# Top-k attention and a leaky-ReLU MLP in one kernel: the softmax chain one step shorter, the grouped PE work in the middle of a step, and eight small token chunks in place of two

## The chip, the cores and the metric

The kernel runs on one core of one Trainium2 chip. The metric is the device time of one execution in microseconds. The engines are named as in the profile: PE (TensorE, matrix products; PEld are its weight loads), DVE (VectorE), ACT (ScalarE), POOL (GpSimd) and SP (SyncE, which issues the DMAs). Each engine works off its own queue in order.

## The reference

For each of 8 batches and 8 heads, with 576 tokens and a head size of 64, every query row keeps its 32 largest scores, the rest are masked, and a softmax weighs the values. The result, as 4608 tokens of 512 numbers, goes through a two-layer MLP with a leaky ReLU.

```python
scores = scale * np.matmul(q, k.transpose(0, 1, 3, 2))          # 8 x 8 x 576 x 576
kth = np.partition(scores, -top_k, axis=-1)[..., -top_k:-top_k + 1]   # top_k = 32
mask = scores >= kth
scores = np.where(mask, scores, -1000000000.0)
scores = scores - np.max(scores, axis=-1, keepdims=True)
attn = np.exp(scores)
attn = attn / (np.sum(attn, axis=-1, keepdims=True) + 1e-09)
attn_out = np.matmul(attn, v)
...
h = x @ w_in                       # x: 4608 x 512, w_in: 512 x 2048
g = np.maximum(0.01 * h, h)
out = g @ w_out                    # w_out: 2048 x 512
```

Attention inputs are float32. The two weight matrices arrive as float64 words, and the kernel turns them into float32 itself.

## The kernel before

**Units and steps.** The attention is cut into 144 units. A unit is 128 query rows of a pair of heads (two row sets of 128 x 576 scores); per batch there are 16 such units and 2 that combine the 64 left-over rows of two pairs. The outer loop (L404) runs over steps. Step s works on unit(s) on DVE and on earlier units on the other engines. The list `steps` holds the first 4 units, then 6 empty steps (the gap, steps 4 to 9), then the remaining 140 units; so unit u from 4 on is worked on at step u + 6, and the last at step 149.

**What happens to a unit.** `scores` (PE L177, 4 matrix products into PSUM tiles psc, copied to s_sb by ACT L186). `top_k` on DVE: four rounds of MAX8 (L195) and three of MATCH_REPLACE8 (L198), two row sets each, cut into four slots, `slot(0)` to `slot(3)`. `mask` on POOL (L207 to L211), one step later. `exponents` and `sums` on ACT (L214, L219), two steps later. `reciprocals` on DVE (L223) and `normalize` on ACT (L226), late in that same step. `transpose_main` and `transpose_tail` on PE (L234, L240) with ACT copies to wT (L235, L241), three steps later (LAG = 3). `weigh_values` on PE (L262, tile po) with ACT copies to the token tiles x (L272), for two units at the end of every even step, between the `scores` of two coming units. s_sb has 6 buffers, psc one of each of its two, the transposes and po share two PSUM buffers.

**The MLP.** Tokens are taken in chunks, two of 128 and then 17 of 256. A chunk is ready when the values of all its units are weighed (`values_at`, `attended`). `mlp` is a generator: for each of 16 blocks of hidden features it multiplies a 128 x 128 block of w_in (stationary) with the x of the chunk (moving, 128 or 256 columns; tile ph, L282), applies the leaky ReLU on ACT into gT (L288), and then multiplies gT (stationary) with w_out (moving, 512 columns; tile pz, L294) per 128 tokens, copies (L301) and stores (L302). Every product in float32 shows as two MATMUL instructions in the profile. All MLP tiles share two PSUM buffers (`ps_ml`).

**The planner.** Everything is emitted in a fixed order (`manual_schedule`). At seven places in a step `mlp_steps(budget)` lets the generator emit pieces of the MLP until their cost, counted in matmul columns, has used up the budget. `slot_budget` sets the budget so that the backlog ends in the step in which the next chunk becomes ready: the MLP of a chunk is spread evenly over the steps until the next one is there.

**The weights.** In the gap DVE converts the sixteen 1 MB pieces of weights with help from ACT (`convert_weights`, L110 to L126); three slots of each gap step start one conversion and finish an older one.

The order of the calls in one step of the kernel before, which the change rearranges, is in the loop at the end of what follows.

Of the kernel before, what the change touches and what calls it, by code (L numbers as in the profile page):

```python
# [8 lines left out]
F32 = mybir.dt.float32  # L9
U32 = mybir.dt.uint32  # L10
AF = mybir.ActivationFunctionType
# [6 lines left out]
def kernel(  # L18
# [27 lines left out]
    WCH = 1024  # L46
    LEFT = S % P
    assert D == 64 and S == 576 and HP == 4 and B % 2 == 0 and LEFT == 64
    CHUNKS = [128] * 2 + [256] * 17
    assert sum(CHUNKS) == B * S  # L50
    CHMAX = max(CHUNKS)
    LOADED, LOADED_V = 6, 5
# [18 lines left out]

    w_in = [const.tile([P, DFF], F32, name=f"w_in{c}") for c in range(HP)]
    w_out = [const.tile([P, 4, DMODEL], F32, name=f"w_out{c}") for c in range(NFC // 4)]
    gT = [const.tile([P, CHMAX], F32, name=f"gT{f}") for f in range(NFC)]

# [135 lines left out]
    def exponents(u, i):  # L213
        nc.scalar.activation(u.s[i], u.s[i], AF.Exp, bias=u.nbias[:, i:i + 1], scale=SCALE,  # L214
                             accum_out=u.z[:, i:i + 1])

    def sums(u):
        u.ze = small.tile([P, 2], F32, name="ze")
        nc.scalar.activation(u.ze, u.z, AF.Copy, bias=1e-9, scale=1.0)  # L219

    def reciprocals(u):
        u.rz = small.tile([P, 2], F32, name="rz")
        nc.vector.reciprocal(u.rz, u.ze)  # L223
# [4 lines left out]
    def transpose_main(u, i):  # L228
        if i == 0:
            u.wT = work.tile([P, 2 * (NKC - 1) + 1, P], F32, name="wT")  # L230
        main = ps_tr.tile([P, 4, P], F32, name="main", tag="tr")
        for c in range(NKC - 1):
            k0 = c * P + i * (S - (NKC - 1) * P)
            nc.tensor.transpose(main[:, c, :], u.s[i][:, k0:k0 + P], ident)  # L234
        nc.scalar.copy(u.wT[:, i * (NKC - 1):(i + 1) * (NKC - 1), :], main)  # L235
# [35 lines left out]
        for o, (pi, _, _) in enumerate(u.outs):  # L271
            nc.scalar.copy(x_of[ch][pi % HP][:, col:col + n], po[:, o, :])  # L272

    def mlp(ch):

        n = CHUNKS[ch]
        t0 = sum(CHUNKS[:ch])
        x = x_of[ch]
        for f in range(NFC):
            ph = ps_ml.tile([P, 512], F32, name="ph", tag="ml")  # L280
            for c in range(HP):
                nc.tensor.matmul(  # L282
                    ph[:, 0:n], w_in[c][:, f * P:(f + 1) * P], x[c][:, 0:n],
                    start=(c == 0), stop=(c == HP - 1),
                )
                if c == 1:
                    yield 2 * max(n, 225)
            nc.scalar.activation(gT[f][:, 0:n], ph[:, 0:n], AF.Prelu, alpha=SLOPE)  # L288
            yield 2 * max(n, 225)
        for r0 in range(0, n, P):  # L290
            m = min(P, n - r0)
            pz = ps_ml.tile([P, 512], F32, name="pz", tag="ml")
            for f in range(NFC):
                nc.tensor.matmul(  # L294
                    pz[0:m, 0:DMODEL], gT[f][:, r0:r0 + m], w_out[f // 4][:, f % 4, :],
                    start=(f == 0), stop=(f == NFC - 1),
                )
                if f % 2 and f + 1 < NFC:
                    yield 2 * DMODEL
            o_sb = work.tile([P, DMODEL], F32, name="o_sb", bufs=1)  # L300
            nc.scalar.copy(o_sb[0:m], pz[0:m, 0:DMODEL])  # L301
            nc.sync.dma_start(out[t0 + r0:t0 + r0 + m, :], o_sb[0:m])  # L302
            yield 2 * DMODEL

    def mlp_cost(ch):
        n = CHUNKS[ch]
        return NFC * HP * max(n, 225) + -(-n // P) * NFC * DMODEL

    ready, running = [], [None]
    backlog, owed = [0.0], [0.0]  # L310
# [15 lines left out]

    LAG = 3

    def values_at(n):

        return n + LAG + (n + LAG) % 2


    FIRST, GAP = 4, 6
# [3 lines left out]
    def unit(n):  # L340
        return steps[n] if 0 <= n < len(steps) else None
# [11 lines left out]
    def attended(s):  # L353
        for at, ch in ready_at:
            if at == s:
                ready.append(ch)
                backlog[0] += mlp_cost(ch)

    def slot_budget(s):

        after = [at for at, _ in ready_at if at >= s]
        until = gap[-1] if s in gap else after[0] if after else s
        return backlog[0] / ((until + 1 - s) * SLOTS)

    SLOTS = 7
    converting, begun = [], [0]

    chunks, raw_chunks = weight_chunks(), []
# [1 line left out]
    def fetch_weights():  # L370
        chunk = next(chunks, None)
        got = load_weights(*chunk) if chunk else None
        if got:
            raw_chunks.append(got)

    def convert():

# [9 lines left out]
    with tc.manual_schedule():  # L387
        last = {p: n for n, u in enumerate(steps) if u for p in u.pairs}
        for p in range(HP):
            load_qk(p)  # L390
            if p < 2:
                scores(units[p])
        for _ in range(3):
            fetch_weights()
        for p in range(HP):
            load_v(p)

        def load_more(s):

            for of, load, n, lag in ((qk_of, load_qk, LOADED, -2), (v_of, load_v, LOADED_V, LAG + 1)):  # L400
                while len(of) < NPAIR and (len(of) < n or last[len(of) - n] + lag <= s):
                    load(len(of))

        for s in range(len(steps) + LAG + 1):  # L404
            cur, old = unit(s), unit(s - 1)
            older, oldest, new = unit(s - 2), unit(s - LAG), ()
            if s % 2 == 0 and s not in gap:
                ahead = units if s < FIRST else steps
                new = ahead[s + 2:s + 4]
            picks = top_k(cur) if cur else iter(())  # L410
            budget = slot_budget(s)

            def slot(n):
                next(picks, None)
                if s in gap and n:
                    convert()

            slot(0)
            if old:
                mask(old, 0)  # L420
                mask(old, 1)
            mlp_steps(budget)
            if older:
                exponents(older, 0)
            if oldest:
                transpose_main(oldest, 0)
            mlp_steps(budget)
            if older:
                exponents(older, 1)
                sums(older)  # L430
            slot(1)
            if oldest:
                transpose_main(oldest, 1)
            mlp_steps(budget)
            if oldest:
                transpose_tail(oldest)
            slot(2)
            mlp_steps(budget)
            if older:
                reciprocals(older)  # L440
            mlp_steps(budget)
            slot(3)
            if older:
                normalize(older, 0)
                normalize(older, 1)
            for u in new[:1]:
                scores(u)
            if s % 2 == 0:
                for u in (unit(s - LAG - 1), oldest):
                    if u:  # L450
                        weigh_values(u)
            for u in new[1:]:
                scores(u)
            mlp_steps(budget)
            mlp_steps(budget)
            attended(s)
            if s >= gap[-1]:
                load_more(s)
        mlp_steps(1e9)
# [53 lines left out]
```

## Time and profile before

| | |
|---|---|
| median of 3 runs | 1662.97 us (1662.88 to 1663.42) |
| profiled execution, its own time | 1659.36 us |
| span of the profiled execution, first to last instruction | 1657.7 us |
| PE busy | 1537.6 us (93%) |
| DVE busy | 1488.3 us (90%) |
| POOL, ACT busy | 1081.0 us (65%), 1011.1 us (61%) |
| mean granted PE clock | 0.965 |
| MAX8 and MATCH_REPLACE8, mean of one | 746 and 743 ns |
| hidden layer ph, 256 columns | 2176 instructions, 509.3 us busy |
| hidden layer ph, 128 columns | 256 instructions, 42.5 us busy |
| output layer pz, 512 columns | 1152 instructions, 527.4 us busy |
| POOL mask, first and second operation | 2220 and 1415 ns |

The profiled execution is 3.6 us below the median of the timed runs. Busy time of PE is the time from the first to the modelled end of overlapping matmuls; how fast PE really works is read from the starts of successive groups in the timeline. "idle before ... <-" names the engine and line whose result ended a wait.

### The profile page before, as it was taken

To read this page: it belongs to the slowest core of one execution; us is meant where nothing else is said; L and a number is where in the kernel's file an instruction comes from. 1 tells how busy PE (TensorE), PEld (TensorE's weight loads), DVE (VectorE), ACT (ScalarE), POOL (GpSimd) and SP (SyncE) were. 2 spreads that over 40 slices of the span, in tenths; PEclk is the share of its full clock that TensorE was granted. 3 is DMA by queue.
4 is the path that set the end of the run, shared out by engine and by line. 5 is a ranking of instruction groups with operands and counts; after the bars stand their busy time and mean duration, and the time that the engine had idled before them with its cause. 6 is when DMAs were issued, how large, how long until landed. Compare 5 with 4: busy or idle time off the path is not lost.

```text
span 1657.7 us, 25822 instructions
## 1 busy us (share of the span) xinstructions
PE 1537.6 (93%) x9360; PEld 1070.1 (65%) x9360; DVE 1488.3 (90%) x3114; ACT 1011.1 (61%) x2277; POOL 1081.0 (65%) x726
## 2 busy tenths in 40 slices
PE   4265679999999999999999999999999999999999
PEld 2252465857576767676767676767676767676764
DVE  8999999999999999999999999999999999999800
ACT  2872566666565757575756666666666666666630
POOL 5204777777777777777777777777777777777700
PEclk9577789999999999999999999999999999999999
DMA  4351010100110010101010010101110010100000
GB/s 165 128 202 43 1 48 17 33 14 30 42 33 14 1 46 25 46 1 42 30 45 1 14 58 13 33 14 30 42 33 14 1 42 1 38 1 14 1 13 13
DMA packets 22463, 57.22 MB, mean 35 GB/s; under 512 B 2368, under 2 KB 2368, under 8 KB 21312
## 3 DMA queue, kind: packets, MB, share of 16 engines
q1 hardware_dynamic: 22336, 55.58, 9.8%
q8 instruction: 73, 1.20, 0.3%
q14 instruction: 54, 0.44, 0.1%
HBM read 46.14 MB, written 9.44 MB: 34 GB/s over the span
## 4 chain that ended last, share of the span: by engine, by line
PE 84%; DVE 14%; ACT 2%; issue 0%; DMA 0%; SPq 0%; ACTq 0%
PE ph L282 29%; PE pz L294 29%; PE po L262 9%; PE psc L177 9%; PE main L234 7%; DVE tops L195 6%; DVE rest L198 5%; PE tail L240 1%; DVE ex L124 1%; DVE w_in L126 1%; DVE ex L110 0%; DVE w_in L122 0%; DVE w_out L126 0%; DVE w_out L122 0%; ACT raw L120 0%; ACT s_sb L226 0%
## 5 line engine op out<-in xcount | busy, mean ns | idle before, releaser
L209 POOL TENSOR_SCALAR pen<-s_sb,tops 128x576 f32<-128x576 f32 x288 | 639.3, 2220 | 369.6 <-DVE tops L195 150.7
L195 DVE MAX8 tops<-rest 128x8 f32<-128x576 f32 x864 | 608.2, 746 | 0.0
L282 PE MATMUL ph<-x,w_in 128*128 128x256 f32 (+1 forms) x2432 | 551.9, 375 | 15.8 <-ACT gT L288 10.9
L294 PE MATMUL pz<-w_out,gT 128*128 128x512 f32 x1152 | 527.4, 598 | 0.0
L282 PEld LDWEIGHTS ph<-x,w_in 128*128 128x128 f32 x2432 | 435.7, 196 | 87.7 <-issue 21.7
L198 DVE MATCH_REPLACE8 rest<-tops,rest 128x576 f32<-128x576 f32 x576 | 423.5, 743 | 0.0
L211 POOL TENSOR_TENSOR s_sb<-s_sb,pen 128x576 f32<-128x576 f32 x288 | 407.4, 1415 | 24.0
L294 PEld LDWEIGHTS pz<-w_out,gT 128*128 128x128 f32 x1152 | 206.7, 191 | 221.3 <-issue 219.6
L226 ACT ACTIVATE s_sb<-s_sb,rz 128x576 f32<-128x576 f32 x288 | 206.9, 768 | 86.7 <-DVE rz L223 86.6
L177 PE MATMUL psc<-kt,qt 64*128 64x288 f32 (+1 forms) x1280 | 199.4, 451 | 61.8 <-ACT s_sb L186 57.3
L235 ACT COPY wT<-main 128x512 f32<-128x512 f32 x288 | 166.0, 577 | 145.3 <-PE main L234 145.2
L214 ACT ACTIVATE s_sb<-s_sb,nbias 128x576 f32<-128x576 f32 x288 | 222.3, 772 | 12.5 <-POOL s_sb L211 12.5
L288 ACT ACTIVATE gT<-ph 128x256 f32<-128x256 f32 (+1 forms) x304 | 112.9, 373 | 177.7 <-PE ph L282 177.1
L186 ACT COPY s_sb<-psc 128x576 f32<-128x576 f32 x288 | 169.5, 640 | 77.9 <-PE psc L177 76.4
L198 DVE MATCH_REPLACE8 rest<-tops,s_sb 128x576 f32<-128x576 f32 x288 | 211.7, 743 | 0.0
L195 DVE MAX8 tops<-s_sb 128x8 f32<-128x576 f32 x288 | 202.0, 743 | 6.6 <-ACT s_sb L186 6.6
L234 PEld LDWEIGHTS main<-ident,s_sb 128*128 128x128 f32 x1152 | 144.8, 146 | 84.3 <-issue 37.5
L234 PE MATMUL main<-ident,s_sb 128*128 128x128 f32 x1152 | 169.0, 282 | 31.8 <-ACT s_sb L226 25.3
L177 PEld LDWEIGHTS psc<-kt,qt 64*128 64x128 f32 (+1 forms) x1280 | 109.3, 185 | 133.4 <-ACT s_sb L186 66.5
L262 PEld LDWEIGHTS po<-wT,vt 128*64 128x64 f32 x3200 | 161.2, 139 | 34.2 <-issue 26.9
L262 PE MATMUL po<-wT,vt 128*64 128x128 f32 (+1 forms) x3200 | 177.8, 268 | 5.2 <-ACT wT L235 5.2
L223 DVE RECIPROCAL rz<-ze 128x2 f32<-128x2 f32 x144 | 23.1, 160 | 86.2 <-ACT ze L219 86.2
(33 smaller groups left out, 491.0 us busy)
## 6 DMA issues: line engine op xcount, KB each, us to landing
vt<-in_vk_dram SPq DMA_DIRECT2D x32, 320.0 KB, 3.5
qt<-in_qT_dram SPq DMA_DIRECT2D x32, 288.0 KB, 3.5
kt<-in_kT_dram SPq DMA_DIRECT2D x32, 288.0 KB, 4.0
out_dram<-o_sb SPq DMA_DIRECT2D x36, 256.0 KB, 2.0
raw<-in_moe_w_in_dram SPq DMA_DIRECT2D x8, 1024.0 KB, 5.3
raw<-in_moe_w_out_dram SPq DMA_DIRECT2D x8, 1024.0 KB, 4.9
```

The costliest lines, as they stand in the source:

```text
L177: nc.tensor.matmul(ps[i][r0:r0 + u.rows, half, 0:HS], qt[d, u.q0:u.q0 + u.rows], kt[d, half * HS:(half + 1) * HS], start=True, stop=True,)
L186: nc.scalar.copy(u.s[i].rearrange("p (h n) -> p h n", h=2), ps[i][:, :, 0:HS])
L195: nc.vector.max(out=u.tops[:, i, r, :], in_=src[i])
L198: nc.vector.match_replace(out=rest[i], in_to_replace=u.tops[:, i, r, :], in_values=src[i], imm_value=LOWEST)
L209: nc.gpsimd.tensor_scalar(pen, u.s[i], u.tops[:, i, ROUNDS - 1, 7:8], MASKED, ALU.is_lt, ALU.mult)
L211: nc.gpsimd.tensor_tensor(u.s[i], u.s[i], pen, ALU.add)
L214: nc.scalar.activation(u.s[i], u.s[i], AF.Exp, bias=u.nbias[:, i:i + 1], scale=SCALE, accum_out=u.z[:, i:i + 1])
L226: nc.scalar.activation(u.s[i], u.s[i], AF.Copy, bias=0.0, scale=u.rz[:, i:i + 1])
L234: nc.tensor.transpose(main[:, c, :], u.s[i][:, k0:k0 + P], ident)
L262: nc.tensor.matmul(po[side * D:(side + 1) * D, o, :], vt[:, c, side, :], u.wT[:, c + side * (NKC - 1) if c + 1 < NKC else 2 * (NKC - 1), r ...
L282: nc.tensor.matmul(ph[:, 0:n], w_in[c][:, f * P:(f + 1) * P], x[c][:, 0:n], start=(c == 0), stop=(c == HP - 1),)
L294: nc.tensor.matmul(pz[0:m, 0:DMODEL], gT[f][:, r0:r0 + m], w_out[f // 4][:, f % 4, :], start=(f == 0), stop=(f == NFC - 1),)
```

## The change

The change touches the order inside a step, the chunks and the MLP of a chunk of 128 tokens.

- **Chain.** LAG goes from 3 to 2. `exponents` and `sums` move from two steps after `top_k` to one, `reciprocals` and `normalize` to the head of the second step, before `slot(0)`, and the transposes into that step. Scores and values of two units are now grouped in the middle of odd steps (after `slot(2)`), where they stood at the end of even steps. Three units' scores are made before the loop where it was two. The seven MLP places are spread anew, and `slot_budget` gives odd steps 0.71 of the mean share and even steps 1.29.
- **Chunks.** Eight chunks of 128 tokens and then 14 of 256. Both kernels have a chunk boundary at token 1024, and 256-token chunks from there on.
- **MLP of 128 tokens.** `hidden_of_tile` keeps x stationary and moves 512 columns of w_in (tile pr); the leaky ReLU writes one half of the single tile gT, four 128 x 128 PE transposes per 512 features turn it (tile pg), and ACT copies it into the other half. The last turn comes inside the output layer. pr, pg and pz share the two PSUM buffers.
- **Weights.** `need_weights` emits conversions as soon as an MLP piece needs them.
- **Costs.** The planner counts n columns per product, without the floor of 225, and 65 for each transpose.

```diff
-    CHUNKS = [128] * 2 + [256] * 17
+    CHUNKS = [128] * 8 + [256] * 14
...
-    gT = [const.tile([P, CHMAX], F32, name=f"gT{f}") for f in range(NFC)]
+    gT = const.tile([P, NFC, CHMAX], F32, name="gT")
...
+    TRANSPOSE = 65
+    def hidden_of_tile(x):
+        left = []
+        def turn(j):
+            pg = ps_ml.tile([P, 4, P], F32, name="pg", tag="ml")
+            for f in range(4):
+                nc.tensor.transpose(pg[:, f, :], gT[:, 4 * j + f, P:2 * P], ident)
+            nc.scalar.copy(gT[:, 4 * j:4 * j + 4, 0:P], pg)
+        for j in range(NFC // 4):
+            pr = ps_ml.tile([P, 512], F32, name="pr", tag="ml")
+            need_weights(HP * (512 * j // WCH + 1))
+            for c in range(HP):
+                nc.tensor.matmul(
+                    pr, x[c][:, 0:P], w_in[c][:, 512 * j:512 * (j + 1)],
+                    start=(c == 0), stop=(c == HP - 1),
+                )
+                if c == 1:
+                    yield 2 * 512
+            nc.scalar.activation(gT[:, 4 * j:4 * j + 4, P:2 * P],
+                                 pr.rearrange("p (f n) -> p f n", f=4), AF.Prelu, alpha=SLOPE)
+            yield 2 * 512
+            if left:
+                turn(left.pop())
+                yield 4 * TRANSPOSE
+            left.append(j)
+        return lambda: turn(left.pop())
...
             for f in range(NFC):
+                need_weights(HP * DFF // WCH + f // 2 + 1)
                 nc.tensor.matmul(
...
+                if f == 3 and last_turn:
+                    last_turn()
+                    yield 4 * TRANSPOSE
...
-        return NFC * HP * max(n, 225) + -(-n // P) * NFC * DMODEL
+        return NFC * (HP * n + n // P * DMODEL + TRANSPOSE * (n == P))
...
-    LAG = 3
+    LAG = 2
     def values_at(n):
-        return n + LAG + (n + LAG) % 2
+        return n + LAG + (n + LAG + 1) % 2
...
+    GROUPED = 0.71
     def slot_budget(s):
...
-        return backlog[0] / ((until + 1 - s) * SLOTS)
+        mean = backlog[0] / ((until + 1 - s) * SLOTS)
+        if s in gap or until < s + 2:
+            return mean
+        return mean * (GROUPED if s % 2 else 2.0 - GROUPED)
...
+    def need_weights(n):
+        while (raw_chunks or converting) and begun[0] - len(converting) < n:
+            convert()
...
-            if p < 2:
+            if p < 3:
                 scores(units[p])
...
-            cur, old = unit(s), unit(s - 1)
-            older, oldest, new = unit(s - 2), unit(s - LAG), ()
-            if s % 2 == 0 and s not in gap:
-                ahead = units if s < FIRST else steps
-                new = ahead[s + 2:s + 4]
+            cur, old, older, new = unit(s), unit(s - 1), unit(s - LAG), ()
+            if s % 2 and s not in gap:
+                new = (units if s < FIRST else steps)[s + 2:s + 4]
```

The body of a step after the change, in the order of emission:

```python
            if older:
                reciprocals(older)
                normalize(older, 0)
                normalize(older, 1)
            slot(0)
            if old:
                mask(old, 0)
                mask(old, 1)
            mlp_steps(budget)
            mlp_steps(budget)
            if older:
                transpose_main(older, 0)
            slot(1)
            mlp_steps(budget)
            if older:
                transpose_main(older, 1)
                transpose_tail(older)
            mlp_steps(budget)
            if old:
                exponents(old, 0)
            slot(2)
            for u in new[:1]:
                scores(u)
            if s % 2:
                for u in (unit(s - LAG - 1), older):
                    if u:
                        weigh_values(u)
            for u in new[1:]:
                scores(u)
            mlp_steps(budget)
            mlp_steps(budget)
            if old:
                exponents(old, 1)
                sums(old)
            slot(3)
            mlp_steps(budget)
```

## The prediction

> **What bounds the kernel now.** I read the slices of the page and the line of the chain first, then busy time by stage, then the timeline of single engines.
>
> ```profile
> PE   4265679999999999999999999999999999999999
> DVE  8999999999999999999999999999999999999800
> PEclk9577789999999999999999999999999999999999
> PE 84%; DVE 14%; ACT 2%; issue 0%; DMA 0%; SPq 0%; ACTq 0%
> ```
>
> DVE is full from the start, PE only from the eighth slice. The chain that ended last lies on DVE at first and on PE from then on. So the time is the moment when PE fills up plus the PE work left. Busy time by stage, PE first and DVE third of the engines, the granted PE clock after them:
>
> ```profile
> 134.00:201.70 67.70, 33.70 (x185) 21.67 (x183) 67.70 (x146) 28.23 (x62) 45.59 (x32) 0.70 0.08 27
> 201.70:284.70 83.00, 70.02 (x496) 50.54 (x497) 81.94 (x178) 50.87 (x127) 63.92 (x43) 0.88 0.09 29
> 367.20:449.70 82.50, 82.50 (x490) 57.25 (x489) 78.00 (x169) 53.26 (x122) 59.92 (x41) 1.00 0.11 36
> 449.70:532.30 82.60, 82.60 (x490) 57.30 (x489) 78.09 (x169) 53.28 (x122) 60.01 (x41) 1.00 0.08 23
> ```
>
> The first two stages are bound by DVE, the later ones by PE: 82.5 us for 256 tokens, eight steps of 10.31. In the second stage a chunk of 128 tokens has to last for eight steps, until the first chunk of 256 is ready, and PE idles. Timeline of PE:
>
> ```profile
> 202.40 2.82 PE L177 MATMUL psc<-kt,qt 64*128 64x288 f32 x8 [4.56 <-ACT s_sb L186]
> 208.64 2.40 PE L282 MATMUL ph<-x,w_in 128*128 128x128 f32 x20
> 210.91 0.66 PE L234 MATMUL main<-ident,s_sb 128*128 128x128 f32 x4
> 269.71 3.60 PE L294 MATMUL pz<-w_out,gT 128*128 128x512 f32 x8
> 273.15 1.04 PE L234 MATMUL main<-ident,s_sb 128*128 128x128 f32 x8
> 276.40 1.24 PE L177 MATMUL psc<-kt,qt 64*128 64x288 f32 x8
> 532.50 1.03 PE L282 MATMUL ph<-x,w_in 128*128 128x256 f32 x4
> ```
>
> From start to next start: pz takes 3.44/8 = 0.43 us, a 128-column ph 2.27/20 = 0.114. psc takes 1.24 on a warm PE and 2.82 after an idle stretch. 532.50 is my anchor: the first product of the tokens from 1024 on, which both kernels compute in chunks of 256. Timelines of DVE and ACT:
>
> ```profile
> 171.09 0.15 DVE L223 RECIPROCAL rz<-ze 128x2 f32<-128x2 f32 x1
> 180.79 0.15 DVE L223 RECIPROCAL rz<-ze 128x2 f32<-128x2 f32 x1
> 171.28 1.44 ACT L226 ACTIVATE s_sb<-s_sb,rz 128x576 f32<-128x576 f32 x2 [1.30 <-DVE rz L223]
> 182.33 1.16 ACT L186 COPY s_sb<-psc 128x576 f32<-128x576 f32 x2
> 20.44 0.78 ACT L214 ACTIVATE s_sb<-s_sb,nbias 128x576 f32<-128x576 f32 x1 [3.44 <-POOL s_sb L211]
> 24.23 0.78 ACT L214 ACTIVATE s_sb<-s_sb,nbias 128x576 f32<-128x576 f32 x1 [2.92 <-POOL s_sb L211]
> ```
>
> A DVE-bound step is 9.70 us, reciprocal included. POOL hands the masked rows of the first unit (DVE done at 17.1) to ACT 3.3 and 7.1 us later.
>
> **The change, part by part.** Everything below runs to the anchor; what follows it is the same work in both kernels.
>
> *The new wait.* Before, the reciprocal stood three slots into a step, for an exponent made early in that step. After, it heads the step, so all MAX8 of the step queue behind it on DVE. The exponent it waits for is the last attention work on ACT in the step before. In odd steps it stands there behind the copies of both new units' psc and of po, thus behind the whole PE group. From the reciprocal of an odd step, at T: normalize lets PE start at T+1.0; transposes, psc and po took from 172.11 to 179.5 in the trace (7.4); the second psc 1.2, its copies 1.2, exponent 0.9, sum 0.2: T+11.9 against 9.7. Cost 2.2 each for steps 13 and 15. Step 3 is colder (psc 2.83, po 4.07 at 37 to 55 us): with everything at those prices T+15.4, with a PE that warms up on the way T+13.0; I take 4.2, nearer to the warmer end, since its work is in one piece. Steps 1 and 11 have scores only: POOL 3.3, exponent 0.9, copies 1.2, psc 2.8, copies 1.2, exponent and sum 1.1 make T+10.5, 0.8 each. Even steps have none: POOL 7.1 and 1.1 end at 8.2.
>
> *The gap.* ACT now normalizes, copies wT and makes unit 3's exponents between the first two conversions (1.1 us per operation). DVE waits about 1.2 for the first conversion's ACT half and 1.6 for the reciprocal that heads step 5. Later MLP operations stand between conversions on ACT: 1.2, at one place. Bounds of all waits before step 10: 0 and 14; I take 0.8 + 4.2 + 2.8 + 1.2 = 9.0. Step 10 began at 133.8. Step 16 begins at 133.8 + 9.0 + 6 x 9.70 + 0.8 + 4.4 = 206.2.
>
> *What the shorter chain brings.* Chunk 1 is released at the end of step 15 instead of 16: 9.7 us sooner. PE reaches it 2.3 before step 16 (exponent and copies follow its last psc), then waits 1.7 for the normalize of step 16.
>
> *Six chunks of 128, steps 16 to 39.* Per chunk 32 pr and 32 pz of 0.43 (27.5), 16 turns at the transposes' 0.11 (1.8), attention of four units at 3.3 (psc 1.17, transposes 1.0, po 1.15), switching 0.4: 42.9, against 41.2 for half a 256 chunk. pr, pg and pz share two PSUM buffers: twice a pr or pz follows one turn of 0.44 while a leaky ReLU (0.6 and 0.2 until it starts) empties its buffer, and the next chunk's first pr waits 0.8 for the copy of pz. Bounds 0 and 3; with some pieces apart I take 1.3. So 44.2, or 11.05 per step: PE-bound, 265.2 in all. PE starts at 206.2 - 2.3 + 1.7 = 205.6 and is through at 470.8. Copies and leaky ReLUs (4.7 us per chunk) fit on ACT (61%).
>
> Here a rule of the Trainium skill stands against the trace. The page TensorE: Matmul & The Clock Gate (Back-to-back issue gap) gives sustained spacings of 81 ns at 128 columns and 131 ns at 512. By it, as an estimate, pr would take 4.2 us per chunk where ph took 10.4; the six chunks would run at DVE's pace, and the sum would come out near 1657. The trace has 114 ns and 430 ns for float32, 14.5 and 13.8 us per chunk; it decides.
>
> *The thin stretch, steps 40 to 47.* Chunk 8 has 256 tokens and is ready at the end of step 47. The changed instruction order indeed spreads chunk 7 alone over these eight steps: PE has 30 + 8 x 3.3 = 57 us of work for 8 x 9.70 = 77.6. The idle stretch of before is not gone, it has moved. DVE is the bound again, so the wait of the odd steps costs again: with MLP pieces between, T+10.2 warm and T+12.4 cold; 0.5 to 2.7, and psc after idling was cold in the same situation of before, so 2.0, four times: 8.0 (0 to 12). Chunk 8 starts 2.0 before step 48: 470.8 + 77.6 + 8.0 - 2.0 = 554.4, 21.9 after the anchor.
>
> The same page (Part 1, the clock gate) says that the clock halves after an idle window of about 3.4 us. PE's idle pieces here are about 2.6 us. By that rule alone PE would stay warm, the 8.0 would be 2.0, and the sum 6 us lower.
>
> *After the anchor.* One psc more is left: 1.2. In steady state the chain from an odd step's first transpose through psc, po, exponent, DVE's 9.70 and the next odd normalize is about 20.4, the PE work of a pair of steps 20.6. PE stays the bound by a hair, and MLP pieces of 0.86 us move it by up to one piece: bounds 0 and 12 over 52 pairs, I take 3. DVE's end has room: after the last MAX8 at 1568 PE had 85 us of work left. At nothing I cost the single gT tile (its readers on PE come in the old order, behind the same leaky ReLUs), the third early psc (PE is idle then; without that cover 2.8 us) and POOL's masks, whose order on POOL is unchanged and which wait for the same MAX8. SP's queue only follows: the number of output stores is the same 36, and they stand between loads that are issued steps ahead of their use.
>
> *Sum.* 21.9 + 1.2 + 3.0 = +26.1. The profiled span 1657.7 (1659.4 with what lies around it, 3.6 below the median) becomes 1683.8; against the median 1663.0 + 26.1 = 1689. Waits make 34.7 of it (9.0 + 5.2 + 1.7 + 7.8 + 8.0 + 3.0); without them it is -8.6, or 1654. With all at their upper bounds it is 1723.
>
> **Rivals.**
> 1. *The waits are hidden.* If ACT gets the late exponents through and PE stays warm, the earlier chunk 1 shows: 1654. For it: DVE idled only 1.1 of 83 us in the second stage. Against: ACT is in order, and behind psc the exponent has no other way. It decides where all waits stay under 8.6, a quarter of mine. 12%.
> 2. *The steady state slips.* Half a us lost in each of 52 pairs makes 26 in place of 3: 1712. For it: 20.4 against 20.6. Against: the planner gives odd steps fewer pieces. 10%.
> 3. *The 128-token form frees PE*, so that steps 16 to 39 run at 9.70: 32 us less, 1657. For it: one pr has a quarter of the weight loads per token. Against: 0.114 and 0.43. 4%.
>
> **How the numbers follow.** The forecast has 74%. A measurement of this kernel can tell about 0.2% (3.3 us) from no change. Rival 1 ends half under and half within it, rival 3 under it, and a thin edge of the forecast within: faster 0.11, same 0.07, slower 0.82. The range reaches down to rival 1 and up to the forecast with most waits at their upper bounds, short of rival 2: 1654 to 1708.
>
> **What would show it.** Waits of the reciprocal for ze of about 2 us or more after steps 3, 13 and 15, and DVE gaps in steps 41 to 47; step 10 near 143, chunk 1's first pr near 204, PE full until about 471, then eight steps with a third of PE idle; ph of chunk 8 near 554; then 82.5 per 256 tokens. Wrong if chunk 8 starts before 535, or if a pair of steps there takes over 21 us.

## The result, and the profile after

The changed kernel takes 1720.17 us (median of 4 runs, 1719.70 to 1721.5) against 1662.95 for the kernel before (4 runs, 1662.88 to 1663.42): a ratio of 1.0345 with a 95% interval of 1.0327 to 1.0363, 57 us slower. The forecast was slower, 1689, with a range up to 1708: the sign was right, the size was less than half. The profiled execution has a span of 1717.8 us, 60.1 more than before.

From the page of the changed kernel, the slices and the chain that ended last:

```profile
PE   4454799999977999999999999999999999999999
DVE  8999988888888999999998989999989899999910
PEclk9686899999989999999999999999999999999999
PE 75%; DVE 16%; ACT 8%; DMA 1%; issue 0%; SPq 0%; ACTq 0%; DVEq 0%
```

PE is full from the sixth slice, one slice sooner than before (there it is the seventh, which the prediction counts as the eighth), has the new thin place at slices 12 and 13, and seems full from then on. But the chain has changed: ACT was 2% of it and is 8%. DVE, which had 9 in almost every slice, shows 8 again and again to the end. So something other than PE's own work seems to hold PE up.

Busy time by stage of the changed kernel; the columns after the window and its length are PE, PEld, DVE, ACT and POOL, then the granted PE clock:

```profile
133.00:193.50 60.50, 27.90 (x172) 18.50 (x170) 59.24 (x125) 26.56 (x57) 37.60 (x26) 0.65 0.09 30
193.50:469.80 276.30, 265.36 (x1483) 146.67 (x1482) 237.49 (x509) 170.54 (x374) 184.13 (x123) 1.00 0.08 25
469.80:556.00 86.20, 67.52 (x377) 39.66 (x376) 76.75 (x166) 51.12 (x110) 56.60 (x39) 0.90 0.09 26
556.00:1658.70 1102.70, 1086.23 (x6641) 743.06 (x6640) 995.98 (x2144) 692.87 (x1586) 769.10 (x514) 1.00 0.07 23
```

And the same 13 chunks of 256 tokens in the kernel before:

```profile
532.50:1598.50 1066.00, 1066.00 (x6634) 739.95 (x6633) 979.48 (x2112) 683.13 (x1579) 758.09 (x507) 1.00 0.07 23
```

The stages of the first fence are the wait for chunk 1, six chunks of 128 tokens, the thin stretch and the chunks from token 1024 on. The last one is the surprise. The same tokens in the same chunk size, at a granted clock of 1.00 in both, take 1102.7 instead of 1066.0: 84.8 per 256 tokens in place of 82.0. (From first product to first product, the first twelve of these chunks take 85.4 and 82.5 on average. The thirteenth, in which the attention ends, takes 78.4 and 75.5.) PE was busy all through the window before; now 16.5 us of it are idle, and another 20 are groups that stand on PE while a product in them waits.

Milestones on PE in the changed kernel, with the forecast beside them in the text:

```profile
193.48 1.98 PE L305 MATMUL pr<-w_in,x 128*128 128x512 f32 x4
...
479.25 1.79 PE L234 MATMUL main<-ident,s_sb 128*128 128x128 f32 x8 [2.75 <-ACT s_sb L226]
480.83 0.42 PE L240 MATMUL tail<-ident,s_sb 128*128 128x128 f32 x1
481.19 2.17 PE L177 MATMUL psc<-kt,qt 64*128 64x288 f32 x8
...
489.46 1.98 PE L305 MATMUL pr<-w_in,x 128*128 128x512 f32 x4 [0.25 <-ACT gT L311]
...
556.05 1.89 PE L282 MATMUL ph<-x,w_in 128*128 128x256 f32 x8
```

Chunk 1 starts at 193.5 (forecast 205.6 with its wait, 12.1 us too late). The six chunks take 276.3 (forecast 265.2, 11.1 too few), the thin stretch 86.3 from start to start (forecast 83.6). So chunk 8 starts at 556.05, where 554.4 was forecast. That looks like a hit, and is luck: three errors that cancel. After it 1161.8 us are left, where the kernel before had 1125.2: 36.6 more, for which the forecast had 4.2.

The waits of the kernel before (us in total, times, the longest):

```profile
DVE rz L223 <- ACT ze L219: 86.2, 64, 10.2
PEld main L234 <- ACT s_sb L226: 26.3, 4, 14.7
PEld tail L240 <- ACT wT L235: 4.7, 12, 0.7
```

The same waits in the changed kernel:

```profile
DVE rz L223 <- ACT ze L219: 148.4, 89, 8.1
PEld main L234 <- ACT s_sb L226: 118.5, 108, 12.5
PEld tail L240 <- ACT wT L235: 27.1, 70, 0.5
```

Three waits in a ring: the reciprocal waits for the exponents, the first transpose for the normalize, and the tail transpose for the copy of the main one. Before, PE's weight load (PEld) had to wait for a normalize 4 times in the whole run; now 108 times. (PE itself stood idle at a main for it 4 times, 25.3 us, and now 31 times, 78.1 us.) The longest waits for the normalize lie ahead of token 1024. After token 1024 the list of the kernel before has neither of the last two waits at all. The changed kernel has, from 556.0 to 1658.7:

```profile
PEld main L234 <- ACT s_sb L226: 38.0, 78, 1.9
PEld tail L240 <- ACT wT L235: 17.0, 44, 0.5
```

To put numbers on it I added up, for all groups of instructions on PE after token 1024, the time from a group's start to the next one's, by pairs of neighbours, and took before from after. From the mains to the tail it is +18.6 (104 times, 0.18 each on average), from an MLP product to the main transpose +13.7, everything else about +4. Counted by single products, 13.8 of the 18.6 stand at the tail itself, at 44 of the 104, and the rest between the mains.

How one odd step runs in steady state is seen in the changed kernel's timeline of DVE,

```profile
1025.31 0.17 DVE L223 RECIPROCAL rz<-ze 128x2 f32<-128x2 f32 x1 [1.69 <-ACT ze L219]
1035.03 0.15 DVE L223 RECIPROCAL rz<-ze 128x2 f32<-128x2 f32 x1
1046.87 0.17 DVE L223 RECIPROCAL rz<-ze 128x2 f32<-128x2 f32 x1 [2.05 <-ACT ze L219]
1056.59 0.15 DVE L223 RECIPROCAL rz<-ze 128x2 f32<-128x2 f32 x1
```

of PE,

```profile
1036.64 1.04 PE L234 MATMUL main<-ident,s_sb 128*128 128x128 f32 x8
1037.92 0.33 PE L240 MATMUL tail<-ident,s_sb 128*128 128x128 f32 x1 [0.24 <-ACT wT L235]
1038.08 1.88 PE L333 MATMUL pz<-w_out,gT 128*128 128x512 f32 x4
1039.90 1.21 PE L177 MATMUL psc<-kt,qt 64*64 64x288 f32 x16
1041.04 2.40 PE L262 MATMUL po<-wT,vt 128*64 128x128 f32 x40
1043.38 1.22 PE L177 MATMUL psc<-kt,qt 64*64 64x288 f32 x16
```

and of ACT:

```profile
1035.21 1.44 ACT L226 ACTIVATE s_sb<-s_sb,rz 128x576 f32<-128x576 f32 x2 [2.84 <-DVE rz L223]
...
1044.66 1.18 ACT L186 COPY s_sb<-psc 128x576 f32<-128x576 f32 x2 [0.90 <-PE psc L177]
1045.72 0.79 ACT L214 ACTIVATE s_sb<-s_sb,nbias 128x576 f32<-128x576 f32 x1
...
1046.63 0.20 ACT L219 ACTIVATE ze<-z 128x2 f32<-128x2 f32 x1
```

The reciprocal at 1035.03 lets ACT normalize, PE transpose (with 0.24 lost at the tail), give 1.8 us to the MLP, then make scores, values and scores; ACT copies the last scores, makes the exponent that stands behind them, the sum comes at 1046.63, and the next reciprocal at 1046.87: 11.84 after the one before. The even step after it takes DVE's 9.72. Together 21.6 here; over the twelve chunks the pair takes 85.4 / 4 = 21.3 (from reciprocal to reciprocal 11.4 for the odd step, between 10.2 and 12.5, and 9.9 for the even one). PE's own work for a pair is 82.5 / 4 = 20.6. The ring is longer than PE's work, so it should set the pace; e5 tests that.

### The profile page after: what moved, and what is told of

The parts are those of the page before. It is cut to its first block, busy times and chain, and to the rows that moved or that the text cites. A ratio compares the mean times of both kernels' runs of the same rounds, so it can differ in the third digit from the quotient of the medians.

```text
span 1717.8 us, 25394 instructions
## 1 busy us (share of the span) xinstructions
PE 1569.1 (91%) x9104; PEld 1022.0 (59%) x9104; DVE 1490.6 (87%) x3114; ACT 1032.9 (60%) x2261; POOL 1079.3 (63%) x726
## 4 chain that ended last, share of the span: by engine, by line
PE 75%; DVE 16%; ACT 8%; DMA 1%; issue 0%; SPq 0%; ACTq 0%; DVEq 0%
PE pz L333 24%; PE ph L282 20%; PE po L262 10%; PE psc L177 10%; DVE tops L195 6%; PE main L234 6%; DVE rest L198 5%; PE pr L305 4%; ACT s_sb L226 2%; ACT wT L235 2%; PE tail L240 2%; ACT s_sb L214 1%; ACT s_sb L186 1%; DVE ex L124 1%; ACT gT L311 1%; DVE ex L110 1%
## 5 line engine op out<-in xcount | busy, mean ns | idle before, releaser
L333 PE MATMUL pz<-w_out,gT 128*128 128x512 f32 x1152 | 526.7, 601 | 13.8 <-DVE w_out L126 7.3
L282 PE MATMUL ph<-x,w_in 128*128 128x256 f32 x1792 | 410.9, 381 | 0.0
L282 PEld LDWEIGHTS ph<-x,w_in 128*128 128x128 f32 x1792 | 331.7, 190 | 56.2 <-issue 16.6
L333 PEld LDWEIGHTS pz<-w_out,gT 128*128 128x128 f32 x1152 | 212.5, 193 | 243.2 <-issue 223.0
L234 PE MATMUL main<-ident,s_sb 128*128 128x128 f32 x1152 | 177.5, 286 | 78.4 <-ACT s_sb L226 78.1
L234 PEld LDWEIGHTS main<-ident,s_sb 128*128 128x128 f32 x1152 | 141.0, 146 | 166.0 <-ACT s_sb L226 118.5
L177 PE MATMUL psc<-kt,qt 64*128 64x288 f32 (+1 forms) x1280 | 192.8, 447 | 22.1 <-ACT s_sb L186 17.8
L262 PE MATMUL po<-wT,vt 128*64 128x128 f32 (+1 forms) x3200 | 177.8, 268 | 4.6 <-ACT wT L235 4.6
L262 PEld LDWEIGHTS po<-wT,vt 128*64 128x64 f32 x3200 | 161.2, 139 | 34.4 <-issue 20.0
L177 PEld LDWEIGHTS psc<-kt,qt 64*128 64x128 f32 (+1 forms) x1280 | 105.7, 185 | 82.2 <-issue 37.9
L288 ACT ACTIVATE gT<-ph 128x256 f32<-128x256 f32 x224 | 84.9, 379 | 102.7 <-PE ph L282 101.0
```

Of the source, the lines that this page charges most:

```text
L177: nc.tensor.matmul(ps[i][r0:r0 + u.rows, half, 0:HS], qt[d, u.q0:u.q0 + u.rows], kt[d, half * HS:(half + 1) * HS], start=True, stop=True,)
L262: nc.tensor.matmul(po[side * D:(side + 1) * D, o, :], vt[:, c, side, :], u.wT[:, c + side * (NKC - 1) if c + 1 < NKC else 2 * (NKC - 1), r ...
L282: nc.tensor.matmul(ph[:, 0:n], w_in[c][:, f * P:(f + 1) * P], x[c][:, 0:n], start=(c == 0), stop=(c == HP - 1),)
L333: nc.tensor.matmul(pz[:, 0:DMODEL], gT[:, f, r0:r0 + P], w_out[f // 4][:, f % 4, :], start=(f == 0), stop=(f == NFC - 1),)
```

## The experiments

Two questions were open. Does the loss come from the step order, in each of the steps (theory S), or from the eight small chunks? And in the step order: from the ring alone, or from the wait at the tail as well (theory T)? All times of e1 to e12 are against the kernel before on the same chips (1660.8 to 1661.0); the first row is that of the result. "Excess" is the ratio less 1, times 1661. The last column is the mean of the first twelve chunks of 256 tokens from token 1024 on, between their first products on PE.

| kernel | median us | ratio to before (95%) | excess us | us per 256 tokens after 1024 |
|---|---|---|---|---|
| changed kernel | 1720.2 | 1.0345 (1.0327 to 1.0363) | 57 | 85.4 |
| e1_two_small_chunks | 1697.3 | 1.0216 (1.0201 to 1.0232) | 36 | 85.0 |
| e2_old_step_order | 1674.1 | 1.0078 (1.0063 to 1.0093) | 13 | 82.5 |
| e3_tail_apart | 1703.4 | 1.0252 (1.0237 to 1.0267) | 42 | 84.5 |
| e4_small_chunks_old_form | 1713.8 | 1.0317 (1.0300 to 1.0334) | 53 | 85.3 |
| e5_early_exponent | 1693.9 | 1.0195 (1.0180 to 1.0210) | 32 | 84.5 |
| e6_early_exponent_tail_apart | 1670.9 | 1.0057 (1.0040 to 1.0074) | 9 | 83.3 |
| e7_both_edits_two_small_chunks | 1661.2 | 0.9999 (0.9989 to 1.0008) | 0 | 83.4 |
| e8_share_0_86 | 1655.2 | 0.9961 (0.9948 to 0.9974) | -6 | 82.9 |
| e9_equal_shares | 1651.5 | 0.9941 (0.9926 to 0.9956) | -10 | 82.5 |
| e10_tail_behind_scores | 1678.0 | 1.0100 (1.0083 to 1.0117) | 17 | 84.4 |
| e11_equal_shares_alone | 1718.5 | 1.0346 (1.0328 to 1.0363) | 57 | 85.0 |
| e12_repaired_eight_chunks | 1665.6 | 1.0028 (1.0017 to 1.0039) | 5 | 82.6 |

### The step order with the old chunks

```diff
-    CHUNKS = [128] * 8 + [256] * 14
+    CHUNKS = [128] * 2 + [256] * 17
```

> The changed kernel with the chunks of before (two of 128 tokens, then 17 of 256); the new order of the step stays. Theory S (the order of the step costs, chunk by chunk, in every steady stretch): chunk 1 starts at 193.5 as in the changed kernel, lasts 86 us as its thin stretch did, then three chunks of 256 at 85.4 us lead to token 1024 at about 536 instead of 556; after that the same 1162 us. Span about 1698, 20 us under the changed kernel, still 2% above before. Theory C (the small chunks and their form are the main cause, and disturb what follows): below 1675, and less than 84 us per 256 tokens.

Measured 1697.3, excess 36, with 85.0 per 256 tokens. The slow pace is there without the small chunks. Theory S holds.

### The chunks with the old step order

The loop, LAG, the shares and the two early scores of the kernel before, with the chunks and the MLP of the changed one:

```diff
-    LAG = 2
+    LAG = 3
...
-        return mean * (GROUPED if s % 2 else 2.0 - GROUPED)
+        return backlog[0] / ((until + 1 - s) * SLOTS)
...
             if older:
-                reciprocals(older)
-                normalize(older, 0)
-                normalize(older, 1)
...
+            if older:
+                exponents(older, 0)
+            if oldest:
+                transpose_main(oldest, 0)
...
-            if s % 2:
-                for u in (unit(s - LAG - 1), older):
+            if s % 2 == 0:
+                for u in (unit(s - LAG - 1), oldest):
```

> The kernel of before in the order of its step (LAG of 3, groups at the end of even steps, even shares), with the eight small chunks, the stationary tokens and the weights on demand of the changed kernel. Theory S: 82.5 us per 256 tokens after token 1024 again, and small chunks at 43 to 44.5 us; chunk 1 starts at about 206, token 1024 at 206 + 6 x 44 + 79 = 549; span about 1674, 1% above before. Theory C: the stretch after token 1024 stays above 84 us per 256 tokens, span above 1690.

Measured 1674.1, excess 13. The pace after token 1024 is the old 82.5; a small chunk takes 42.6 to 44.6, the thin stretch 80.4. So the step order alone costs 36 and the chunks alone 13; the 8 us that are missing to 57 arise where both meet, most of them in the small chunks: the new order costs the six of them 14.0 (276.3 against 262.3), and the three chunks of 256 with the same tokens 6.8 (254.6 in e1 against 247.8 before).

### An MLP place between main and tail

```diff
             if older:
                 transpose_main(older, 1)
-                transpose_tail(older)
             mlp_steps(budget)
+            if older:
+                transpose_tail(older)
```

> The changed kernel with one edit: the tail transpose comes after the next place for MLP pieces instead of directly behind the main transposes. Theory T (PE waits at the tail for a PSUM buffer that ACT has not emptied; 18.6 us after token 1024 and some 10 us before it, and PE is the bound): the waits between main and tail shrink to a third, the span drops by 15 to 28 us, to 1690 to 1702. Theory L (the loop of reciprocal, normalize, PE group, exponent and top-k is the bound, and PE only waits at another place): the waits move to the first main transpose, and the span changes by less than 5 us.

Measured 1703.4: the excess falls from 57 to 42. The tail's wait is all but gone, as these waits of the kernel show:

```profile
DVE rz L223 <- ACT ze L219: 132.8, 83, 8.1
PEld main L234 <- ACT s_sb L226: 122.8, 111, 12.4
PEld tail L240 <- ACT wT L235: 6.8, 20, 0.5
```

Counted by single products, PE loses 5 us between a main and the tail in the whole run, where it lost 22 (2.8 and 13.8 of them after token 1024), and a small chunk from the third on takes 44.1 to 44.4 instead of 45.5 to 45.8. Theory T holds: the tail stood where its PSUM buffer was still being emptied by ACT, and the MLP product that had covered that was moved away by the change. 15 us of the time came back, 10.6 of them after token 1024. The main transposes now wait slightly longer (122.8 against 118.5): the ring of exponent, reciprocal and normalize is still there.

### The old form of the 128-token MLP

```diff
-        if n == P:
+        if False:
             last_turn = yield from hidden_of_tile(x_of[ch])
...
-        return NFC * (HP * n + n // P * DMODEL + TRANSPOSE * (n == P))
+        return NFC * (HP * n + n // P * DMODEL + 0)
```

> The changed kernel with the chunks of 128 tokens computed in the old form (w_in stationary, 128 columns of tokens moving, no turns of gT); chunk 0 then begins when all of w_in is converted. By the prediction's terms a chunk loses 1.8 us of turns and 1 us of waits for PSUM and gains 0.7 us of narrower products: about 2 us on each of the six PE-bound chunks, 12 us in all, span about 1706. If the wider form is the better one on PE, as the planner's floor of 225 columns said, the span grows by 30 us or more.

Measured 1713.8, excess 53 in place of 57. A small chunk takes 44.6 with w_in stationary and 45.5 with the tokens stationary: the new form is about 1 us per chunk worse, where about 2 were expected. It is no gain, and a small part of the loss.

### The exponent before the second scores

In odd steps the second row set's exponent and the sums move ahead of the second new unit's scores; the ring becomes shorter by one psc (1.2) and its copies on ACT (1.2).

```diff
+            if old and new:
+                exponents(old, 1)
+                sums(old)
             for u in new[1:]:
                 scores(u)
             mlp_steps(budget)
             mlp_steps(budget)
-            if old:
+            if old and not new:
                 exponents(old, 1)
                 sums(old)
```

> The changed kernel with one edit: in odd steps the second exponent and the sum are emitted before the scores of the second new unit, so they no longer stand on ACT behind that unit's copies. Theory L (a loop of reciprocal, normalize, PE group, exponent and 9.7 us of top-k sets the period, 21.2 us per pair of steps): the waits of the reciprocal fall from 148 us to under 60, the period after token 1024 falls from 85.2 to about 84.2 us (the waits at the tail stay), the thin stretch and the start lose some 8 us; span down 15 to 22 us, near 1700. Theory P (only PE's own waits count, the loop has slack): the reciprocals wait less, but the span changes by less than 6 us.

Measured 1693.9: the excess falls from 57 to 32, more than the 15 to 22 us expected. ACT in an odd step of this kernel:

```profile
1024.39 0.78 ACT L214 ACTIVATE s_sb<-s_sb,nbias 128x576 f32<-128x576 f32 x1
...
1025.29 0.20 ACT L219 ACTIVATE ze<-z 128x2 f32<-128x2 f32 x1
1025.40 1.18 ACT L186 COPY s_sb<-psc 128x576 f32<-128x576 f32 x2
```

The sum stands ahead of the copy of the second scores now. The thin stretch shrinks from 86.3 to 77.5, about DVE's eight steps of 9.70; of its reciprocals only one still waits for long (1.8 us). Of the 25 us, 10 lie after token 1024, 9 in the thin stretch and 6 ahead of it. The waits of this kernel:

```profile
DVE rz L223 <- ACT ze L219: 125.3, 71, 8.1
PEld main L234 <- ACT s_sb L226: 81.4, 70, 12.1
PEld tail L240 <- ACT wT L235: 30.1, 72, 0.5
```

The sum of the reciprocal's waits did not fall as far as expected (125.3). DVE is not the bound in steady state, so what it no longer waits for at one reciprocal it may well wait for at another. The waits of main for the normalize went from 118.5 to 81.4, after token 1024 from 38.0 (78 times) to 16.0 (41 times). The tail's wait stays.

### Both edits together

The edits of e3 and e5 in one kernel:

```diff
             mlp_steps(budget)
+            if older:
+                transpose_tail(older)
...
+            if old and new:
+                exponents(old, 1)
+                sums(old)
             for u in new[1:]:
                 scores(u)
```

> The changed kernel with both edits, the early exponent and the tail transpose behind an MLP place. Theory L with T: with the loop out of the way, the tail edit brings its whole 1.4 us per 256 tokens and 1.2 us per small chunk: 83 us per 256 tokens, span 1673 to 1682, which leaves little more than the 13 us that the small chunks cost under the old order of the step. If the two waits stand in for one another, the span is that of the better single edit, 1698 to 1704.

Measured 1670.9, excess 9, a little below what was expected with both theories. Apart the edits brought 25 and 15, together 48 of 57. So the ring and the tail account for most of the loss, and each hides part of what the other is worth: with the tail's edit alone the waits of main grew (118.5 to 122.8), with the exponent's alone those of the tail (27.1 to 30.1).

### Both edits with the old chunks

The same, with the chunk line of e1:

```diff
-    CHUNKS = [128] * 8 + [256] * 14
+    CHUNKS = [128] * 2 + [256] * 17
```

> As the run with both edits, but with the two small chunks of before. Chunk 1 is then released 10 us sooner than in the kernel before and nothing else should be left of the cost: 1650 to 1660, just under before. If the shorter chain has a cost that neither edit touches, it stays above 1668.

Measured 1661.2: the time of the kernel before, just outside what was expected. Chunk 2 starts at 271.5, where the kernel before had 284.7, so the shorter chain does bring its gain, 13 us. It is given back over 16 chunks at 83.4 instead of 82.5.

### The shares of odd and even steps

The last kernel (e7) with

```diff
-    GROUPED = 0.71
+    GROUPED = 0.86
```

> Both edits, two small chunks, and odd steps with 0.86 of the mean MLP share instead of 0.71. What is left of the cost after the release of chunk 1 (271.5 against 284.7 us in the kernel before) is 83.4 against 82.5 us per 256 tokens. If it is PE that arrives too early at the transposes of odd steps, more pieces ahead of them and between them help: 82.8 us or less, and 1648 to 1655, under before. If the odd step's group is what makes the loop long, more pieces in it cost: 84 us or more, above 1668.

and with 1.0, which gives every step the same share of the MLP:

> The same with equal shares for odd and even steps. By the first theory at best as with 0.86 (1648 to 1658); by the second clearly worse, 85 us per 256 tokens and above 1685, since an odd step then has 13 us of PE work and an even one 8.

Measured 1655.2, at the edge of what the first theory expected, and 1651.5, inside it. The pace goes from 83.4 over 82.9 to 82.5, that of the kernel before, and chunk 2 still starts at 274.6, 10.1 sooner. Busy time of e9 from token 1024 on, and its waits:

```profile
523.30:1591.60 1068.30, 1067.17 (x6642) 745.46 (x6641) 994.29 (x2137) 687.20 (x1583) 767.22 (x512) 1.00 0.07 23
```

```profile
DVE rz L223 <- ACT ze L219: 78.8, 97, 8.4
PEld main L234 <- ACT s_sb L226: 77.1, 54, 11.8
```

PE is idle for 1.1 us in 1068 (16.5 in the changed kernel). This is the fastest kernel of the study, 0.6% under the one before (ratio 0.9941, 0.9926 to 0.9956). Why equal shares fit better than 0.71 no single line shows; what is shown is that the unequal shares cost 10 us once the two edits were in.

### The tail behind the first scores

In e7's order, the tail moves behind the first new unit's scores in odd steps, so that psc covers the copy.

```diff
-            if older:
+            if older and not new:
                 transpose_tail(older)
...
             for u in new[:1]:
                 scores(u)
+            if older and new:
+                transpose_tail(older)
```

> Both edits, two small chunks, share 0.71, and in odd steps the tail transpose only after the scores of the first new unit, with 1.2 us of PE work between the main transposes and it. The waits between main and tail and at the tail (about 8 us in all after the first chunks) should go in odd steps: 3 to 6 us less than the 1661 of the run with both edits, 1655 to 1658. If the place does not matter any more, 1660 to 1662.

A miss, and in the wrong direction: 1678.0, 17 slower than e7. PE in an odd step of this kernel:

```profile
1003.79 1.21 PE L177 MATMUL psc<-kt,qt 64*64 64x288 f32 x16
1004.93 0.33 PE L240 MATMUL tail<-ident,s_sb 128*128 128x128 f32 x1
1005.19 2.62 PE L262 MATMUL po<-wT,vt 128*64 128x128 f32 x40
```

Now po follows the tail at once and reads the wT that the tail fills. The copy from the tail to wT stands on ACT behind the copies of psc. From tail to po PE loses 0.15 in each of 50 odd steps (7.6). Between the products of po it loses another 9.1 (po's 40 products take 2.55 from the first to the next group, where they took 2.34). That is more than the 12.7 by which the stretch after token 1024 grew against e7; some 4 were gained elsewhere. The waits of po for that copy (PEld po L262 <- ACT wT L241) went from 4.7 us at 12 places in e7 to 12.9 at 58. The edit spared the tail its wait for a buffer and made the tail's reader wait instead.

### Equal shares in the changed kernel alone

The changed kernel with equal shares and nothing else, to tell whether the shares are a cause by themselves.

```diff
-    GROUPED = 0.71
+    GROUPED = 1.0
```

> The changed kernel with equal shares for odd and even steps and nothing else. Theory L (the loop through the odd step's PE group binds as long as the second exponent stands behind the group): an odd step gets 2 us more MLP work per step, most of it between the reciprocal and the exponent, so the loop and the period grow: 86.5 us or more per 256 tokens, span 1725 to 1760. If the share of 0.71 alone was the fault, the span falls by 10 us or more, as it did once the exponent was early (1661 to 1651).

Measured 1718.5, ratio 1.0346: no change, and both expectations missed. Its waits:

```profile
PEld main L234 <- ACT s_sb L226: 146.5, 106, 12.2
PEld tail L240 <- ACT wT L235: 6.5, 20, 0.5
```

The tail's wait is gone as in e3 (27.1 to 6.5), yet the same time has gone to the wait of main for the normalize (118.5 to 146.5). It seems that more MLP in the odd steps lengthens the ring by about what it saves at the tail. In this kernel, moving PE work between odd and even steps changed the place of the waits and not the time.

### The eight small chunks in the best order

The fastest order (e9) with the chunks of the changed kernel:

```diff
-    CHUNKS = [128] * 2 + [256] * 17
+    CHUNKS = [128] * 8 + [256] * 14
```

> Early exponent, tail apart, equal shares, and the eight small chunks of the change: the price of the small chunks in the best order of the step found. Under the order of before they cost 13 us (1674 against 1661); six of them at 44 us in place of 41.3 make 16 us less what an earlier start of the thin stretch gives. 1662 to 1668, at or just above before.

Measured 1665.6, 14 more than e9 (1651.5), with 82.6 per 256 tokens, small chunks of 43.8 to 44.5 (the last 46.1) and a thin stretch of 78.8. The small chunks cost about what they cost in the old order (13). This part of the loss does not depend on the ring.

## Why the prediction was right in sign and wrong in size

**The step that failed is the term "after the anchor", 3.0 with bounds 0 and 12.** It measured 35.4 (36.6 less the one psc of 1.2). Two things were wrong in it.

- *The ring.* It was put at about 20.4 for a pair of steps, against 20.6 of PE work. The trace after has 21.3: 9.9 for the even step and 11.4 for the odd one, for which 20.4 leaves 10.7. What the forecast did not name is in the odd step shown above: 1.8 us of MLP products between tail and psc, and 0.24 at the tail. That is more than the 0.9 missing, so something else in the 20.4, whose terms the prediction does not give, was too large. Rival 2, which named this slip, was given 10% and half a us per pair; it was 0.7 per pair. e5 shows that the ring binds: 25 us back, 10 of them after token 1024, for an exponent that no longer stands behind the second scores. A difference of 0.2 us between two sums with errors of about a us each was no ground for 10%.
- *The tail.* The transposes were priced at 1.0 per unit without a wait. The diff moved the MLP place that had stood between the second main and the tail, and the prediction did not name what that place had covered. It covered the copy that empties the tail's PSUM buffer: PE lost 13.8 us there after token 1024 and 8.3 before it. No rival had it. e3 shows it, with 15 us back.

The trace of the kernel before had a line that showed this wait, at a place where no MLP product was ready to stand in between:

```profile
42.06 0.33 PE L240 MATMUL tail<-ident,s_sb 128*128 128x128 f32 x1 [0.41 <-ACT wT L235]
```

From the first product of the chunk at token 1024 to that of the last chunk the changed kernel takes 1102.7, e3 1092.0, e5 1092.8, e6 with both edits 1077.7, e12 with equal shares on top 1069.1, and the kernel before 1066.0. So the ring and the tail make 25 of the 36.6, and the unequal shares, once both are out of the way, most of the rest; how the shares act stays open.

"Wrong if a pair of steps there takes over 21 us" was the right thing to look at, and it happened. One side sum of the prediction does not come out: with the upper bounds that it gives (14, 18, 12 and 12) and the other waits as they stand it is 1717, not 1723.

**The waits at the start** were priced at 9.0 before step 10 and cost 1.4 (step 10 at 135.2 instead of 133.8). Step 3 was priced at 4.2, which is T+13.9, and ran at T+11.7:

```profile
48.03 0.17 DVE L223 RECIPROCAL rz<-ze 128x2 f32<-128x2 f32 x1 [1.96 <-ACT ze L219]
```

Steps 1 and 11 cost nothing, and the reciprocal in the gap waited 0.6, where the gap was priced at 4.0. Steps 13 and 15, priced at T+11.9, took 11.0 and 10.9. The shorter chain's own gain, 9.7, fits what the repaired kernels show: e7 starts chunk 2 earlier by 13.2, e9 by 10.1.

**The six small chunks** were priced at 44.2 and took 46.0 on average. Twice per chunk the pr or pz behind a turn waits for a PSUM buffer, as forecast (about 0.9 per chunk); the tail's wait (about 1.2 per chunk) was missing. In e3 and e6, which have little of it, the last three chunks take 44.0 to 44.1, in e12 most take 43.8 to 44.5. The first two chunks were 1.1 and 2.1 longer than the later four: in them mains behind a pr or pz waited for a normalize, 1.5 us in all in the first and 3.0 in the second, which the later four do not show. For the form of the MLP, e4 puts the new one 0.9 per chunk above the old one. The products themselves, pr at 0.43 and the old ph at 0.113, came out as read from the trace before. The spacing of 131 ns at 512 columns in the Trainium skill (TensorE: Matmul & The Clock Gate, Back-to-back issue gap) does not hold for these float32 products: the trace after has 0.43 us for pr.

**The thin stretch** moved to steps 40 to 47, as read from the changed order, and took 2.7 more than forecast. PE did run cold there: after an idle piece of 2.75 us the eight mains lasted 1.79 us and psc 2.17, where warm ones last 1.04 and 1.24, and the stage has a granted clock of 0.90. In e5 the stretch is 77.5, so most of the extra was the waits of the odd steps, as the forecast said.

**Rivals 1 and 3** fell. The waits were not hidden, and the 128-token form did not free PE. Rival 2 was the one that came, with 35 us in place of its 26.

## What to carry to other kernels

When two bounds are within a few per cent of each other, as here a ring of 20.4 and PE work of 20.6, don't take the one that is larger by a hair: add up every instruction inside the ring, the products that a planner may put there too, and give the other side a large chance. For every piece that a change moves away from between two instructions, ask what it covered; here a transpose right behind two others, with two PSUM buffers for all of them, waited for a copy, some 0.3 us at a time, and 15 us of the loss came back with one MLP place in between. A predicted milestone that is hit shows little by itself; compare each stage before it with its own forecast.

## What the runs showed of the hardware

PE lost clock after a short idle piece. In the thin stretch of the changed kernel PE was idle for 2.75 us up to 479.25, and the transposes and scores after it lasted 1.7 times as long as warm ones (1.79 against 1.04, 2.17 against 1.24). The granted clock, the third number from the end, was full up to that piece and fell at its end:

```profile
476.00:479.20 3.20, 0.50 (x2) 0.00 (x0) 3.20 (x8) 1.15 (x5) 1.34 (x1) 1.00 0.00 0
479.20:483.00 3.80, 3.75 (x17) 2.50 (x17) 3.80 (x9) 2.77 (x7) 3.62 (x3) 0.56 0.00 0
```

The Trainium skill (TensorE: Matmul & The Clock Gate, Part 1) speaks of a free-running idle window of about 3.4 us. Here 2.75 us of idle time were enough, so the prediction's estimate by that rule, a PE that stays warm with idle pieces of about 2.6 us, is not safe to plan with.

PE's share of busy time hides a wait that is part of a group. In the window after token 1024 PE was busy for 98.5%, and the window was still 3.4% longer than in the kernel before. The starts of successive groups and the list of waits showed the loss, the busy share did not.
